# Loads of q, k and v issued by GpSimd and cast by the transfer, in an attention and feed-forward kernel

## The chip, the cores and the metric

The kernel runs on one core of one Trainium2 chip. The metric is the time of one execution on the device in microseconds (us); less is better. The core has five engines that run their own instruction streams in order and meet at semaphores: PE (matrix products), DVE (vector), ACT (activations), POOL (GpSimd) and SP (sync). DMA engines, shared by all of them, move the data; a transfer is issued by an instruction on one of the engines.

## The reference

Eight batches of eight heads, 576 tokens, 64 elements a head. Attention has a bias from a running sum of `s`, a causal mask, and is followed by a layer norm and a two-layer feed-forward block with a residual.

```python
scores = scale * np.matmul(q, k.transpose(0, 1, 3, 2))
cum = np.cumsum(np.maximum(s, 0.0), axis=-1)
bias = -(cum[:, :, :, None] - cum[:, :, None, :])
scores = np.where(causal, -1000000000.0, scores + np.minimum(bias, 0.0))
attn = softmax(scores)
x = np.matmul(attn, v)                      # (8, 8, 576, 64) -> (8, 576, 512)
xn = (x - mu) / np.sqrt(var + 1e-06) * g_ln
out = x + np.maximum(xn @ w_ch1, 0.0) @ w_ch2
```

Inputs and output are float32; inside, the kernel works in bfloat16 for the products.

## The kernel before

The order of all work is written out by hand; nothing reorders it. The main loop runs over 64 heads, n = 8 * batch + head. In each head it does four things: `pre(n)` issues loads, casts and transposes for heads to come; `scores(b, h)` makes the transposed scores of one head with PE (`sa`, `sb`, `sc`), takes their exponential on ACT into `er`, and has POOL zero what the causal mask hides (`affine_select`, four of 128 x 128 a head, and a smaller one for two heads in `scores_d`); `pv` multiplies the exponentials of the head before with `v` into `pot`; and between these stand units of the feed-forward block of the batch before (`run_units`), 32 `ph` and `py` units a batch. The attention stages thus fill in between the large matrix products, and the two share PE.

A head's scores need q and k with the 64 head elements on the partitions. Four heads make a group, numbered gam (two in a batch); a group's q and k lie in `qT[gam % 2]` and `kT[gam % 2]`. Batches 0 and 1 (`NPE` is 2) are loaded by token blocks, cast into tiles of the pool `pairs` and transposed on PE. Batches 2 to 7, groups 4 to 15, go another way, in three steps for k and three for q:

- `ld_rows(kind, gam, part)` loads token rows of four heads as float32 into a staging tile, from the sync queue. Part 0 holds three tiles of 128 tokens; part 1 one of 128 and one of 64.
- `cast_rows` has POOL cast each tile into one of six row buffers, `rows[turn % 6]` (128 tokens x 4 heads x 128 columns of bfloat16), and copy four bias columns beside the 64 elements (from `cTk` or `cTq`).
- `tr_rows` issues one transposing DMA a row buffer from the sync queue, out of `rows` into `kT` or `qT`.

`v` is loaded from the sync queue into `vtmp` and cast by `cast("v", ...)` into `v_bf[b % 2]`, in five tiles a batch, the last of 64 tokens.

The sync queue also issues the weights' loads in the first heads and the stores of `out`. All loads, transposes and stores of batches 2 to 7 therefore stand in the sync queue in the order in which `pre` writes them, and all casts stand in POOL's queue between the selects of the mask. In the steady part, `pre` spreads the three steps over four heads:

```python
elif n >= 16:
    gam = n // 4 + 1
    if n % 4 == 0:
        tr_rows("k", gam, 0)
        cast_rows("q", gam, 0)
        ld_rows("q", gam, 1)
    elif n % 4 == 1:
        tr_rows("q", gam, 0)
        cast_rows("k", gam, 1)
        ld_rows("k", gam + 1, 0)
```

and so on for the two other heads. The feed-forward weights `w2` are cast by POOL at heads 12 to 14 (`cast_w2`), those of `w1` by DVE.

Of the kernel before, what the change touches and what calls it, by code (L numbers as in the profile page):

```python
# [9 lines left out]
F32 = mybir.dt.float32  # L10
BF16 = mybir.dt.bfloat16
# [4 lines left out]
P = 128  # L16
# [3 lines left out]
def kernel(  # L20
# [11 lines left out]
    nc = tc.nc  # L32
    B, H, S, D = q.shape
# [5 lines left out]
    NF = S // P  # L39
    NT = NF + 1  # L40
    TL = S - NF * P
# [4 lines left out]
    EW = 1664  # L46
    G = 4
    NPE = 2
    PARTS = ((0, 1, 2), (3, 4))
    QT = 6  # L50
    QP = S // QT

    const = ctx.enter_context(tc.tile_pool(name="const", bufs=1))
    stage = ctx.enter_context(tc.tile_pool(name="stage", bufs=2))
    pairs = ctx.enter_context(tc.tile_pool(name="pairs", bufs=3))
    wst = ctx.enter_context(tc.tile_pool(name="wst", bufs=4))
    small = ctx.enter_context(tc.tile_pool(name="small", bufs=4))
    xpool = ctx.enter_context(tc.tile_pool(name="xpool", bufs=3))
# [41 lines left out]

    def load_v(b, t):
        pn = P if t < NF else TL
        tmp = stage.tile([P, H, D], F32, name="vtmp", tag="vtmp", bufs=3)
        nc.sync.dma_start(
            out=tmp[:pn], in_=v[b, :, t * P : t * P + pn, :].rearrange("h s d -> s h d")
        )
        return tmp

    def copy_on(eng, out, in_):
        if eng == "act":  # L110
            nc.scalar.copy(out=out, in_=in_)
        elif eng == "dve":
            nc.vector.tensor_copy(out=out, in_=in_)
        else:
            nc.gpsimd.tensor_copy(out=out, in_=in_)  # L115

    loaded = {}
# [10 lines left out]
    def cast(kind, b, i, eng):  # L128
        if b >= B:
            return  # L130
        tmp = loaded.pop((kind, b, i))
        if kind == "v":
            pn = P if i < NF else TL
            copy_on(eng, v_bf[b % 2][:pn, i, :, 0:D], tmp[:pn])
        else:
            t = pairs.tile([P, QT, 2, D], BF16, name=kind + "p", tag=kind + "p")
            copy_on(
                eng,
                t[0:QP].rearrange("p t h d -> p h t d"),
                tmp[0:QP].rearrange("p h (t d) -> p h t d", d=D),  # L140
            )
            ready[kind, b, i] = t
# [45 lines left out]
    def bias_rows():  # L188
# [7 lines left out]
        for t0, t1, pn in ((0, NF, P), (NF, NT, TL)):  # L196
# [5 lines left out]
                out=cTq[0:pn, t0:t1, :, 3], in0=tr[0:pn, 0, t0:t1, :], scalar1=-1.0  # L202
            )

    def ld_rows(kind, gam, part):
        if gam >= 2 * B:
            return
        src = k if kind == "k" else q
        b, h0 = gam // 2, (gam % 2) * G
        tmp = stage.tile([P, 3, G, D], F32, name=kind + "tmp", tag=kind + "tmp")  # L210
        for u, t in enumerate(PARTS[part]):
            pn = P if t < NF else TL
            nc.sync.dma_start(
                out=tmp[0:pn, u],
                in_=src[b, h0 : h0 + G, t * P : t * P + pn, :].rearrange("h s d -> s h d"),
            )
        loaded[kind, gam, part, "rows"] = tmp

    turn = [0]

    def cast_rows(kind, gam, part):
        if gam >= 2 * B:
            return
        tmp = loaded.pop((kind, gam, part, "rows"))
        got = []
        for u, t in enumerate(PARTS[part]):
            pn = P if t < NF else TL
            r = rows[turn[0] % 6]
            turn[0] += 1
            nc.gpsimd.tensor_copy(out=r[0:pn, :, 0:D], in_=tmp[0:pn, u])  # L230
            nc.gpsimd.tensor_copy(
                out=r[0:pn, :, D:KA],
                in_=(cTk if kind == "k" else cTq)[0:pn, t, gam * G : (gam + 1) * G, :],
            )
            got.append((t, pn, r))
        ready[kind, gam, part, "rows"] = got

    def tr_rows(kind, gam, part):
        if gam >= 2 * B:
            return  # L240
        dst = (kT if kind == "k" else qT)[gam % 2].rearrange("p h s -> p (h s)")
        for t, pn, r in ready.pop((kind, gam, part, "rows")):
            nc.sync.dma_start_transpose(  # L243
                out=dst[:, t * G * P : t * G * P + G * pn].rearrange(
                    "p (h s) -> p h s", h=G
                ),
                in_=r[0:pn].rearrange("p h c -> p (h c)"),
            )
# [293 lines left out]
    for i in range(2):  # L542
# [43 lines left out]
    def pre(n):  # L586
        b, h = n // H, n % H
# [74 lines left out]
            if 3 <= h and b + 1 < B:  # L662
                cast("v", b + 1, h - 3, "pool")

        if n == 10:
            ld_rows("k", 4, 0)
        elif n == 11:
            ld_rows("q", 4, 0)
        elif n == 12:
            cast_rows("k", 4, 0)  # L670
            ld_rows("k", 4, 1)
        elif n == 13:
            tr_rows("k", 4, 0)
            cast_rows("q", 4, 0)
            ld_rows("q", 4, 1)
            ld_rows("k", 5, 0)
        elif n == 14:
            tr_rows("q", 4, 0)
            cast_rows("k", 4, 1)
            ld_rows("q", 5, 0)  # L680
        elif n == 15:
            tr_rows("k", 4, 1)
            cast_rows("q", 4, 1)
            tr_rows("q", 4, 1)
            cast_rows("k", 5, 0)
            ld_rows("k", 5, 1)
        elif n >= 16:
            gam = n // 4 + 1
            if n % 4 == 0:
                tr_rows("k", gam, 0)  # L690
                cast_rows("q", gam, 0)
                ld_rows("q", gam, 1)
            elif n % 4 == 1:
                tr_rows("q", gam, 0)
                cast_rows("k", gam, 1)
                ld_rows("k", gam + 1, 0)
            elif n % 4 == 2:
                tr_rows("k", gam, 1)
                cast_rows("q", gam, 1)
                ld_rows("q", gam + 1, 0)  # L700
            else:
                tr_rows("q", gam, 1)
                cast_rows("k", gam + 1, 0)
                ld_rows("k", gam + 1, 1)

    NU = {10: 4, 11: 4, 12: 4, 13: 4, 14: 3, 15: 3, 16: 3, 17: 3, 18: 4}

# [82 lines left out]
```

## Time and profile before

| | |
|---|---|
| timed runs | 470.35, 472.9 and 474.61 us; median 472.9 |
| profiled execution | 468.62 us, of which the span from the first to the last instruction is 466.9 |
| granted PE clock, mean | 0.893 |
| PE, DVE, ACT, POOL busy | 371.4, 213.3, 175.4, 193.2 us |
| DMA | 61.09 MB in 167,578 packets, 155,624 of them under 512 bytes |

A profile comes from one execution. In its lists of groups, a row has the kernel's line, the engine, the operation, what it writes and reads by the program's names, sizes, the count; then the busy time in us and the mean of one in ns; then the time that the engine was idle just before, and what ended it ("issue" where the profile shows nothing that was waited for). A row of the timeline has its start and its length in us, and in brackets the idle time before it in us and what released it. SPq is the sync engine's queue: the time of an instruction there is the time to issue a transfer, not to carry it out. A window row has the busy time of PE, PE's weight loads, DVE, ACT and POOL with instruction counts, then the granted PE clock, the mean busy share of the 16 DMA engines, and GB/s.

### The profile page before, as it was taken

Reading aid. Unit: us, or ns where it says so; the run is one execution under the profiler, and the core shown is the slowest. Engines: PE = TensorE matmul, PEld = TensorE weight load, DVE = VectorE, ACT = ScalarE, POOL = GpSimd, SP = SyncE. Lnnn points to the kernel's source line nnn. Section 1 sums busy time; section 2 is a strip of 40 time slices with the busy share of each in tenths; the row PEclk is TensorE's granted clock in tenths of the full one; section 3 lists DMA queues with packets and bytes.
Section 4 is the critical chain, followed back from the end, with each engine's and each line's share of the span. In section 5 each row is a group of like instructions: output and inputs, shape, how many; then the busy total and the mean of one; then the engine's idle time right before and its main releaser. Section 6 shows DMA issues by size and latency. Waiting matters only on the chain. (4 is left out here: it accounts for less than half of the span.)

```text
span 466.9 us, 8307 instructions
## 1 busy us (share of the span) xinstructions
PE 371.4 (80%) x2848; PEld 200.3 (43%) x2895; DVE 213.3 (46%) x525; ACT 175.4 (38%) x339; POOL 193.2 (41%) x609
## 2 busy tenths in 40 slices
PE   1486469917979984999299939896699899999995
PEld 0264335504535542555155515453355455444442
DVE  7579777523714640447024712473145526511211
ACT  4252225603337242643255325532272463050320
POOL 3274516835646625554446545543466222000000
PEclk9975559987979995999789977999599999999999
DMA  7885078985877487665866586549765600101102
GB/s 201 216 249 138 13 251 241 217 181 137 191 146 139 97 176 169 115 129 119 189 135 132 117 196 131 117 103 174 162 133 107 137 2 22 69 0 46 46 23 68
DMA packets 167578, 61.09 MB, mean 131 GB/s; under 512 B 155624, under 2 KB 158768, under 8 KB 167536
## 3 DMA queue, kind: packets, MB, share of 16 engines
q1 hardware_dynamic: 167456, 60.51, 57.1%
q8 instruction: 23, 0.38, 0.4%
q14 instruction: 19, 0.16, 0.1%
q10 hardware_dynamic: 80, 0.05, 0.0%
HBM read 36.85 MB, written 9.44 MB: 99 GB/s over the span
## 5 line engine op out<-in xcount | busy, mean ns | idle before, releaser
L485 PE MATMUL py<-w_bf,hT 128*128 128x512 bf16 x554 | 135.6, 382 | 1.5 <-DVE yo L494 0.4
L467 PE MATMUL ph<-xT,w_bf 128*128 128x512 bf16 x488 | 130.3, 403 | 2.1 <-ACT hT L477 0.5
L328 POOL TENSOR_SCALAR_AFFINE_SELECT er<-er 128x128 bf16<-128x128 bf16 x256 | 73.4, 303 | 87.4 <-ACT er L314 86.9
L314 ACT ACTIVATE er<-sa 128x512 bf16<-128x512 f32 x64 | 38.1, 596 | 166.1 <-PE sa L305 107.3
L477 ACT ACTIVATE hT<-ph 128x512 bf16<-128x512 f32 x108 | 64.5, 597 | 91.9 <-PE ph L467 90.8
L467 PEld LDWEIGHTS <-w_bf 128*128 128x128 bf16 x576 | 53.9, 101 | 58.1 <-issue 11.3
L475 DVE TENSOR_SCALAR hT<-ph 128x512 bf16<-128x512 f32 x36 | 24.9, 692 | 113.7 <-PE ph L467 112.2
L305 PEld LDWEIGHTS <-kT 68*128 68x128 bf16 x464 | 35.8, 105 | 95.2 <-issue 38.2
L305 PE MATMUL sa<-qT,kT 68*128 68x512 bf16 x64 | 27.8, 434 | 60.2 <-DMA qT<-rows 47.3
L485 PEld LDWEIGHTS <-hT 128*128 128x128 bf16 x576 | 51.9, 98 | 50.2 <-issue 2.0
L379 PEld LDWEIGHTS <-er 128*128 128x128 bf16 x960 | 42.7, 105 | 17.9 <-issue 5.2
L379 PE MATMUL pot<-v_bf,er 128*128 128x65 bf16 x960 | 45.1, 203 | 3.2 <-POOL v_bf L115 2.5
L230 POOL CAST rows<-qtmp 128x256 bf16<-128x256 f32 (+1 forms) x60 | 24.1, 401 | 46.8 <-issue 25.1
L387 DVE RECIPROCAL rinv<-pot 128x5 f32<-128x5 f32 x64 | 12.4, 193 | 61.2 <-PE pot L379 61.0
L494 DVE TENSOR_TENSOR yo<-py,xb 128x512 f32<-128x512 f32 x32 | 22.0, 689 | 39.5 <-PE py L485 39.3
L314 ACT ACTIVATE er<-sc 128x512 bf16<-128x512 f32 x64 | 38.9, 608 | 0.0
L314 ACT ACTIVATE er<-sb 128x512 bf16<-128x512 f32 x64 | 38.2, 596 | 1.8 <-PE sb L305 0.7
L230 POOL CAST rows<-ktmp 128x256 bf16<-128x256 f32 (+1 forms) x60 | 23.9, 399 | 25.7 <-DMA kT<-rows 17.3
L305 PE MATMUL sb<-qT,kT 68*128 68x384 bf16 (+2 forms) x176 | 28.4, 269 | 2.5 <-DMA qT<-rows 2.3
L305 PE MATMUL sc<-qT,kT 68*128 68x256 bf16 (+1 forms) x224 | 28.5, 249 | 0.0
L389 DVE TENSOR_TENSOR xb<-pot,rinv 128x256 f32<-128x256 f32 x64 | 27.2, 424 | 2.2
L438 DVE TENSOR_SCALAR xn<-xb,mv,rs 128x512 bf16<-128x512 f32 x32 | 20.6, 704 | 9.7 <-POOL rs L425 9.7
(71 smaller groups left out, 289.8 us busy)
## 6 DMA issues: line engine op xcount, KB each, us to landing
vtmp<-in_v_dram SPq DMA_DIRECT2D x32, 256.0 KB
out_dram<-yo SPq DMA_DIRECT2D x32, 256.0 KB
ktmp<-in_k_dram SPq DMA_DIRECT2D x48, 128.0 KB
qtmp<-in_q_dram SPq DMA_DIRECT2D x48, 128.0 KB
w1tmp<-in_moe_w_ch_dram SPq DMA_DIRECT2D x8, 512.0 KB
w2tmp<-in_moe_w_ch_dram SPq DMA_DIRECT2D x8, 512.0 KB
ktmp<-in_k_dram SPq DMA_DIRECT2D x8, 288.0 KB
qtmp<-in_q_dram SPq DMA_DIRECT2D x8, 288.0 KB
```

What stands on the lines that cost most here:

```text
L230: nc.gpsimd.tensor_copy(out=r[0:pn, :, 0:D], in_=tmp[0:pn, u])
L305: nc.tensor.matmul(dst[:, a0 - q0 : a1 - q0], lhsT=k_cols(b, h, kb), rhs=cols, start=True, stop=True,)
L314: nc.scalar.activation(out=e[:, u, o : o + 512], in_=a, func=ACT.Exp, scale=scale)
L328: nc.gpsimd.affine_select(out=e[:, u, o : o + P], in_=e[:, u, o : o + P], compare_op=ALU.is_ge, fill=0.0, base=0, pattern=[[1, P]], channe ...
L379: nc.tensor.matmul(pot[:, t, :], lhsT=e[:, u, o : o + P], rhs=vv[:, kb, h, :], start=(kb == 0), stop=(kb == last),)
L389: nc.vector.tensor_tensor(out=xb[b][:, :, hs], in0=pot[:, 0:NF, 0:D], in1=rinv[:, 0:NF].unsqueeze(2).to_broadcast([P, NF, D]), op=ALU.mult,)
L438: nc.vector.tensor_scalar(out=xn, in0=x, scalar1=mv[:, t, 0:1], scalar2=rs[:, t : t + 1], op0=ALU.subtract, op1=ALU.mult,)
L467: nc.tensor.matmul(ph, lhsT=w1_bf[:, kd, fb * P : (fb + 1) * P], rhs=xT[:, kd, :], start=(kd == 0), stop=(kd == KD - 1),)
L475: nc.vector.tensor_scalar_max(out=hT[:, fb, :], in0=ph, scalar1=0.0)
L477: nc.scalar.activation(out=hT[:, fb, :], in_=ph, func=ACT.Relu)
L485: nc.tensor.matmul(py[0], lhsT=hT[:, fb, t * P : (t + 1) * P], rhs=w2_bf[:, fb, :], start=(fb == 0), stop=(fb == FB - 1),)
L494: nc.vector.tensor_add(out=yo, in0=py[0], in1=x)
```

## The change

For batches 2 to 7 the loads of q, k and v are issued by GpSimd, with a float32 source and a bfloat16 destination, so that the transfer itself converts. The destination is the row buffer, or `v_bf`. Staging tiles and POOL's casts of these batches fall away; the bias columns are still copied by POOL, right behind each load. There are nine row buffers instead of six, `pairs` has two buffers instead of three, and a group's steps stand in other heads: k part 0 is loaded six heads before the group's first head, q part 0 five, both parts 1 four heads before; the transposes follow two heads after each load. Before, q part 1 was transposed one head before the group, now two.

```diff
+    NR = 9
-    pairs = ctx.enter_context(tc.tile_pool(name="pairs", bufs=3))
+    pairs = ctx.enter_context(tc.tile_pool(name="pairs", bufs=2))
-    rows = [const.tile([P, G, P], BF16, name=f"rows{i}") for i in range(6)]
+    rows = [const.tile([P, G, P], BF16, name=f"rows{i}") for i in range(NR)]
...
     def load_v(b, t):
         pn = P if t < NF else TL
+        if b >= NPE:
+            nc.gpsimd.dma_start(
+                out=v_bf[b % 2][:pn, t, :, 0:D],
+                in_=v[b, :, t * P : t * P + pn, :].rearrange("h s d -> s h d"),
+            )
+            return None
...
         tmp = loaded.pop((kind, b, i))
+        if tmp is None:
+            return
...
     def ld_rows(kind, gam, part):
-        tmp = stage.tile([P, 3, G, D], F32, name=kind + "tmp", tag=kind + "tmp")
-        for u, t in enumerate(PARTS[part]):
+        got = []
+        for t in PARTS[part]:
             pn = P if t < NF else TL
-            nc.sync.dma_start(
-                out=tmp[0:pn, u],
+            r = rows[turn[0] % NR]
+            turn[0] += 1
+            nc.gpsimd.dma_start(
+                out=r[0:pn, :, 0:D],
                 in_=src[b, h0 : h0 + G, t * P : t * P + pn, :].rearrange("h s d -> s h d"),
             )
-    def cast_rows(kind, gam, part):
-            nc.gpsimd.tensor_copy(out=r[0:pn, :, 0:D], in_=tmp[0:pn, u])
             nc.gpsimd.tensor_copy(
                 out=r[0:pn, :, D:KA],
                 in_=(cTk if kind == "k" else cTq)[0:pn, t, gam * G : (gam + 1) * G, :],
             )
...
+        for gam in range(2 * NPE, 2 * B):
+            m = n - 4 * gam
+            if m == -6:
+                ld_rows("k", gam, 0)
+            elif m == -5:
+                ld_rows("q", gam, 0)
+            elif m == -4:
                 tr_rows("k", gam, 0)
+                ld_rows("k", gam, 1)
                 ld_rows("q", gam, 1)
+            elif m == -3:
                 tr_rows("q", gam, 0)
+            elif m == -2:
                 tr_rows("k", gam, 1)
                 tr_rows("q", gam, 1)
```

The lines of the changed kernel are other ones: the row load is at L226, the bias copy at L230, the transpose at L242, the select at L327, the `v` load at L105.

POOL at head 27 (batch 3, head 3), before: the cast of a `v` tile, three casts of k rows with their bias copies, and the four selects of the head.

```order
L115 CAST v_bf_103<-vtmp 128x8x64
L230 CAST rows_109<-ktmp 128x4x64
L231 COPY rows_109<-cTk 128x4x4
L230 CAST rows_110<-ktmp 128x4x64
L231 COPY rows_110<-cTk 128x4x4
L230 CAST rows_111<-ktmp 128x4x64
L231 COPY rows_111<-cTk 128x4x4
L328 AFFINE_SELECT er<-er 128x128 x4
```

POOL at the same head after the change (here `rows_109` to `rows_117` are the nine buffers):

```order
L105 DMA v_bf_103<-in_v_dram 128x8x64
L226 DMA rows_109<-in_q_dram 128x4x64
L230 COPY rows_109<-cTq 128x4x4
L226 DMA rows_110<-in_q_dram 128x4x64
L230 COPY rows_110<-cTq 128x4x4
L226 DMA rows_111<-in_q_dram 128x4x64
L230 COPY rows_111<-cTq 128x4x4
L327 AFFINE_SELECT er<-er 128x128 x4
```

Each cast has become the issue of a transfer, at the same place ahead of the selects. At head 28, after the change, POOL issues one `v` load and four row loads:

```order
L105 DMA v_bf_103<-in_v_dram 128x8x64
L226 DMA rows_112<-in_k_dram 128x4x64
L230 COPY rows_112<-cTk 128x4x4
L226 DMA rows_113<-in_k_dram 64x4x64
L230 COPY rows_113<-cTk 64x4x4
L226 DMA rows_114<-in_q_dram 128x4x64
L230 COPY rows_114<-cTq 128x4x4
L226 DMA rows_115<-in_q_dram 64x4x64
L230 COPY rows_115<-cTq 64x4x4
L327 AFFINE_SELECT er<-er 128x128 x4
L351 AFFINE_SELECT er<-er 64x2x64
```

Both parts 1 of a group stand in one head. `rows_115` is the buffer that held the same group's first k tile; its transpose stands in the sync queue at this head.

The sync queue at heads 32 and 33, before: stores, transposes and loads stand between each other.

```order
L507 DMA out_dram<-yo 128x512
L243 DMA_TRANSPOSE kT_107<-rows_113 128x4x128
L243 DMA_TRANSPOSE kT_107<-rows_114 128x4x128
L243 DMA_TRANSPOSE kT_107<-rows_109 128x4x128
L213 DMA qtmp<-in_q_dram 128x4x64
L213 DMA qtmp<-in_q_dram 64x4x64
L507 DMA out_dram<-yo 128x512
L104 DMA vtmp<-in_v_dram 128x8x64
L243 DMA_TRANSPOSE qT_105<-rows_110 128x4x128
L243 DMA_TRANSPOSE qT_105<-rows_111 128x4x128
L243 DMA_TRANSPOSE qT_105<-rows_112 128x4x128
```

After the change, at the same heads:

```order
L506 DMA out_dram<-yo 128x512
L242 DMA_TRANSPOSE kT_107<-rows_116 128x4x128
L242 DMA_TRANSPOSE kT_107<-rows_117 128x4x128
L242 DMA_TRANSPOSE kT_107<-rows_109 128x4x128
L506 DMA out_dram<-yo 128x512
L242 DMA_TRANSPOSE qT_105<-rows_110 128x4x128
L242 DMA_TRANSPOSE qT_105<-rows_111 128x4x128
L242 DMA_TRANSPOSE qT_105<-rows_112 128x4x128
```

The loads have left the queue; stores and transposes keep their order.

More of the change, by code (lines that the diff above doesn't have):

```diff
@@ L203, in bias_rows @@
             )
+    turn = [0]
     def ld_rows(kind, gam, part):
@@ L209, in ld_rows @@
         b, h0 = gam // 2, (gam % 2) * G
-        tmp = stage.tile([P, 3, G, D], F32, name=kind + "tmp", tag=kind + "tmp")
-        for u, t in enumerate(PARTS[part]):
+        got = []
+        for t in PARTS[part]:
             pn = P if t < NF else TL
-            nc.sync.dma_start(
-                out=tmp[0:pn, u],
+            r = rows[turn[0] % NR]
+            turn[0] += 1
+            nc.gpsimd.dma_start(
+                out=r[0:pn, :, 0:D],
                 in_=src[b, h0 : h0 + G, t * P : t * P + pn, :].rearrange("h s d -> s h d"),
             )
-        loaded[kind, gam, part, "rows"] = tmp
-    turn = [0]
-    def cast_rows(kind, gam, part):
[L222 to L230, printed above, removed]
             nc.gpsimd.tensor_copy(
@@ L663, in pre @@
                 cast("v", b + 1, h - 3, "pool")
[L665 to L689, printed above, removed]
+        for gam in range(2 * NPE, 2 * B):
[5 more added lines that the diff above has]
+            elif m == -4:
                 tr_rows("k", gam, 0)
-                cast_rows("q", gam, 0)
+                ld_rows("k", gam, 1)
                 ld_rows("q", gam, 1)
-            elif n % 4 == 1:
+            elif m == -3:
                 tr_rows("q", gam, 0)
-                cast_rows("k", gam, 1)
-                ld_rows("k", gam + 1, 0)
-            elif n % 4 == 2:
+            elif m == -2:
                 tr_rows("k", gam, 1)
-                cast_rows("q", gam, 1)
-                ld_rows("q", gam + 1, 0)
-            else:
                 tr_rows("q", gam, 1)
-                cast_rows("k", gam + 1, 0)
-                ld_rows("k", gam + 1, 1)
     NU = {10: 4, 11: 4, 12: 4, 13: 4, 14: 3, 15: 3, 16: 3, 17: 3, 18: 4}
```

## The prediction

> **What bounds the kernel now.** I read the page's first part, then the waits of the tensor engine, of GpSimd (POOL) and of the sync queue (SPq), then one stall in the timeline. The page first.
>
> ```profile
> PE 371.4 (80%) x2848; PEld 200.3 (43%) x2895; DVE 213.3 (46%) x525; ACT 175.4 (38%) x339; POOL 193.2 (41%) x609
> ```
>
> No engine is full over the span. PE, at 80%, is nearest, so the question is what its idle fifth waits for. The waits answer that (engine and line, what was waited for, us in total, times, longest).
>
> ```profile
> PE sa L305 <- DMA qT<-rows: 47.3, 8, 10.2
> POOL rows L230 <- issue: 28.9, 8, 5.6
> POOL rows L230 <- DMA qT<-rows: 20.2, 11, 5.7
> POOL rows L230 <- DMA kT<-rows: 17.3, 8, 3.8
> SPq L243 <- POOL er L328: 34.5, 32, 1.8
> SPq L243 <- POOL rows L231: 30.8, 27, 2.3
> ```
>
> Eight times the first score matmul of a group (`sa`) waits for the transposing DMA that writes `qT`: 47.3 us, the largest wait of PE. The rest shows why that DMA is late: POOL's casts into the six row buffers wait for transposes to read those buffers out, and the sync queue's transposes wait for POOL. Each in-order queue holds up the other. The timeline of one stall, at head 36:
>
> ```profile
> 217.51 0.39 POOL L230 CAST rows<-qtmp 64x256 bf16<-64x256 f32 x1 [4.67 <-issue]
> 221.75 2.82 SPq L243 DMA_TRANSPOSE kT<-rows  x2
> 225.65 0.40 POOL L230 CAST rows<-ktmp 128x256 bf16<-128x256 f32 x1 [2.57 <-DMA kT<-rows]
> 227.42 2.70 SPq L243 DMA_TRANSPOSE qT<-rows  x2
> 231.41 0.58 PE L305 MATMUL sa<-qT,kT 68*128 68x512 bf16 x1 [8.61 <-DMA qT<-rows]
> 232.66 1.90 PE L467 MATMUL ph<-xT,w_bf 128*128 128x512 bf16 x4
> 238.84 0.38 PE L305 MATMUL sa<-qT,kT 68*128 68x512 bf16 x1
> 239.50 1.89 PE L467 MATMUL ph<-xT,w_bf 128*128 128x512 bf16 x8
> 241.17 0.54 POOL L328 TENSOR_SCALAR_AFFINE_SELECT er<-er 128x128 bf16<-128x128 bf16 x2 [0.20 <-ACT er L314]
> 243.41 0.38 PE L305 MATMUL sa<-qT,kT 68*128 68x512 bf16 x1
> 245.86 0.62 PE L379 MATMUL pot<-v_bf,er 128*128 128x65 bf16 x15
> ...
> 267.69 0.38 PE L305 MATMUL sa<-qT,kT 68*128 68x512 bf16 x1
> ...
> 279.46 0.59 PE L305 MATMUL sa<-qT,kT 68*128 68x512 bf16 x1 [7.04 <-DMA qT<-rows]
> ```
>
> Three numbers come from it. From 238.84 (head 37) to 267.69 (head 43) are six heads without a stall, 28.85 us, 4.81 each; eight would take 38.5 us. From stall to stall, 231.41 to 279.46, a batch of eight heads takes 48.05. The difference is more than the 7 to 9 us of waiting, because after a stall PE runs slowly for a while: four `ph` matmuls in 1.90 us at 232.66, eight in 1.89 at 239.50. The head after the stall takes 7.43 us where the next takes 4.57, 2.86 more.
>
> **What the change removes.** POOL loses its casts of rows and of `v` (batches 2 to 7). SPq loses those loads, and with them its waits for staging buffers; transposes and stores stay. Nine row buffers instead of six, and loads two heads ahead of their transposes, take the mutual hold-up apart. A row load now waits for a transpose issued one or two heads earlier, with one exception. The 64-partition `q` load of the third step reuses the buffer whose transpose is issued in the same head. That transpose waits for PE to finish the scores of the head before, then takes about 1.4 us on the queue (2.82 for two) and 1.3 to land (230.12 to 231.41). POOL gets there after its four selects, three loads and three copies, later than that, so this wait costs nothing at the price below. What else could be late at a group's first scores is ten transposes at about 1.35, 13.5 us, in the 19.2 us of four heads: they fit, if rows arrive.
>
> **What it adds: POOL writes the transfers itself.** POOL's rows now:
>
> ```profile
> L328 POOL TENSOR_SCALAR_AFFINE_SELECT er<-er 128x128 bf16<-128x128 bf16 x256 | 73.4, 303 | 87.4 <-ACT er L314 86.9
> L230 POOL CAST rows<-qtmp 128x256 bf16<-128x256 f32 (+1 forms) x60 | 24.1, 401 | 46.8 <-issue 25.1 <-DMA qT<-rows 20.2 <-POOL rows L231 1.5
> L230 POOL CAST rows<-ktmp 128x256 bf16<-128x256 f32 (+1 forms) x60 | 23.9, 399 | 25.7 <-DMA kT<-rows 17.3 <-issue 3.8 <-DMA ktmp<-in_k_dram 3.5
> L115 POOL CAST v_bf<-vtmp 128x512 bf16<-128x512 f32 (+1 forms) x36 | 21.9, 612 | 6.4 <-DMA vtmp<-in_v_dram 6.4
> L231 POOL COPY rows<-cTk 128x16 bf16<-128x16 bf16 (+1 forms) x60 | 13.8, 230 | 0.0
> L231 POOL COPY rows<-cTq 128x16 bf16<-128x16 bf16 (+1 forms) x60 | 11.5, 192 | 0.0
> L352 POOL TENSOR_SCALAR_AFFINE_SELECT er<-er 64x128 bf16<-64x128 bf16 x32 | 9.3, 292 | 5.8 <-ACT er L349 5.8
> L425 POOL TENSOR_TENSOR rs<-rs,mhalf 128x4 f32<-128x4 f32 (+1 forms) x8 | 8.7, 1089 | 25.7 <-DVE rs L424 23.0 <-DMA kT<-rows 2.6
> ```
>
> Per batch POOL keeps 73.4/8 = 9.2 of selects, 9.3/8 = 1.2 of small ones, 8.7/8 = 1.1 of powers and (13.8 + 11.5)/6 = 4.2 of bias copies: 15.7 us. It loses 48.0/6 = 8.0 of row casts and about 5 x 0.61 = 3.0 of `v` casts. It gains 25 transfers: 16 row loads of 128 partitions (512 runs of 256 bytes), 4 of 64, 4 `v` loads of 1,024 runs and one of 512.
>
> What such a transfer costs POOL no row shows, so I bound it. The cheap end is what the sync queue takes to issue the same transfer:
>
> ```profile
> 242.39 1.67 SPq L213 DMA_DIRECT2D ktmp<-in_k_dram  x3
> 226.89 0.43 SPq L104 DMA_DIRECT2D vtmp<-in_v_dram  x1
> ```
>
> That is 0.56 for a row load, 0.43 for `v`. For the dear end I let POOL step through every run at its own pace. A cast of 256 elements takes 401 ns and a copy of 16 about 211, so 0.79 ns an element; four elements a run (two addresses and two lengths, my assumption) give 512 x 4 x 0.79 ns + 0.21 = 1.83 us for a row load, 1.02 for one of 64 partitions, 3.45 and 1.83 for `v`. The nearest row is not evident, so I take the geometric middle: 1.01, 0.76, 1.22 and 0.89. The batch adds 16 x 1.01 + 4 x 0.76 + 4 x 1.22 + 0.89 = 25.0 us, and POOL needs **40.7 us a batch**, against the 38.5 that PE needs. The ends are 13.4 (POOL 29) and 49.0 (POOL 65).
>
> The Trainium skill, page "DMA: Bandwidth & Descriptors", section "Specifications", gives about 1 us to the first byte where GpSimd issues and about 0.6 where sync does. Adding that 0.4 to the sync queue's rows would make the 25 transfers 23.4 us, POOL 39.1 and the median about 426, an estimate; no run here shows it.
>
> Behind a POOL transfer stand the selects of the next head, and PE's `pot` waits for those. The cover: head 37's selects end at 241.71 and its `pot` starts at 245.86, 4.15 us later. Heads 2 to 4 of a batch carry a `v` load and three or four row loads each: 6.3, 6.0 and 7.0 us of POOL, 19.4 in the time of three heads, 14.4. POOL falls 5.0 late, 0.85 more than the cover. I take the batch at 40.7 + 0.85, **41.5 us**.
>
> The first stall, at head 16, is another place:
>
> ```profile
> 105.56 0.59 PE L305 MATMUL sa<-qT,kT 68*128 68x512 bf16 x1 [10.22 <-DMA qT<-rows]
> 85.51 3.98 POOL L172 CAST w_bf<-w2tmp 128x1024 bf16<-128x1024 f32 x4
> ```
>
> It costs 10.2 and a slow head, about 13.1. At head 14 POOL will have the four `w2` casts (3.98), three `v` loads (3.7), three row loads with copies (3.7) and its selects (1.4), 12.7 us in a head of about 4; head 15 adds 1.5. Less the cover, PE loses about 6.3. The gain here is 6.8.
>
> **The sum.** Five batches (heads 20 to 60) save 5 x (48.05 - 41.5) = 32.8, the first stall 6.8: 39.6 us. The profiled execution took 468.62 us (466.9 of span); the result is 429.0. That execution lies 4.3 under the median of the timed runs, 472.9, so I predict **433 us** for a median. The extra memsets of three buffers (0.3 each) and the two-deep `pairs` pool fall where POOL waits for ACT (86.9 us in the L328 row); uncovered they cost 1 us.
>
> **The rivals.**
>
> POOL's transfers are cheap (below 0.85 us a row load). Then PE sets the pace and all 47.3 us go, with about 15 of the slow heads (two thirds of eight times 2.86, since short waits cost less): 406, **410** as a median. For it speaks that the sync queue issues the same in 0.56. Chance 0.14.
>
> POOL becomes the bound, and the kernel is slower. The place is POOL's queue in batches 1 to 6, the price what writing 512 or 1,024 runs takes. It breaks even where the 25 transfers take 48.05 - 0.85 - 15.7 = 31.5 us, that is 1.26 times my price, 1.27 us a row load; above that every batch loses. At the dear end 5 x (65 + 0.85 - 48.05) = 89 us are lost and nothing is won at head 16: **about 560**; halfway from the break-even, about 515. For it speaks that rows are short, and so many for each transfer; against it only that POOL has 59% of the span free. Chance 0.25.
>
> The DMA engines become the bound, because a converting packet takes longer.
>
> ```profile
> q1 hardware_dynamic: 167456, 60.51, 57.1%
> 231.00:276.00 45.00, 40.53 (x330) 22.02 (x336) 19.13 (x53) 20.39 (x40) 23.77 (x80) 0.92 0.67 141
> ```
>
> The last row's 0.67 is the DMA share: 32.2 us of a 48.05 us batch. A packet takes 0.571 x 466.9 x 16 / 167456 = 25.5 ns on the mean. Converted per batch: 9,216 row and 4,608 `v` packets. If these took twice as long, 22 us more over 16 engines, a batch would need 54 us: **about 503**. It binds from 1.4 times on and loses from 1.7. Against it: they write half the bytes. Chance 0.10.
>
> POOL is held up by the vector engine. The vector rows that read SBUF with one source:
>
> ```profile
> L438 DVE TENSOR_SCALAR xn<-xb,mv,rs 128x512 bf16<-128x512 f32 x32 | 20.6, 704 | 9.7 <-POOL rs L425 9.7
> L475 DVE TENSOR_SCALAR hT<-ph 128x512 bf16<-128x512 f32 x36 | 24.9, 692 | 113.7 <-PE ph L467 112.2
> ```
>
> If each `xn` shut POOL out while it runs, a batch would gain 20.6/8 = 2.6 us: 44.1, and **446** in all. But `xn`, from SBUF, takes 704 ns where `hT`, from PSUM, takes 692: it runs no faster from there. Chance 0.04. The rule behind it is in the Trainium skill, page "SBUF — State Buffer", section "SBUF: two separate sides": a vector operation in a two-port mode keeps GpSimd from writing its descriptors, so that a transfer issued there seems blocked. By that rule the change is a risk here only if `xn` is in such a mode, and the two durations speak against it.
>
> Last, gain and cost cancel near the break-even price: no change, **473**, chance 0.07.
>
> **How the numbers follow.** Forecast (415 to 455) 0.40, cheap POOL 0.14, vector hold-up 0.04: faster 0.58. Cancelled: 0.07. POOL bound 0.25 and DMA bound 0.10: slower 0.35. A change of 1% either way is about what a measurement of this kernel can tell from none. The range runs from 409, the floor of the cheap case, to 515, the middle of the bound case; left out is the dear half of POOL's price, some 0.15, and a little below. Faster cases alone run from 409 to 455.
>
> **What would show it.** Right: the 47.3 us wait of `sa` falls under 10; POOL's transfers show 0.8 to 1.2 us for 512 runs; POOL is over 85% busy between heads 20 and 60 with its idle before L327 nearly gone; `pot` has a short new wait for the selects. The cheap rival shows POOL still idle for ACT, and heads of 4.6 to 5.1 us throughout. The bound case shows `pot` waiting for selects in nearly every head and sync's transposes waiting for row loads. The DMA case shows row loads landing late after POOL has long issued them. I am wrong first of all if the price of a POOL transfer lies outside 0.85 to 1.25 us.

## The result, and the profile after

The changed kernel takes 442.94 us (median of three, 441.30 to 445.39) against 472.9: the ratio is 0.938, its 95% interval 0.928 to 0.948. The forecast was 433, with a range of 409 to 515. The ratios here leave out the slower executions that a chip shows now and then, so they can differ by half a per cent from the quotient of two medians. The profiled execution took 441.30 us, 439.2 of span, at a mean granted clock of 0.975.

The first part of its page, and the two large rows of the list of DMA queues (packets, MB, share of 16 engines):

```profile
PE 367.5 (84%) x2848; PEld 199.3 (45%) x2895; DVE 215.0 (49%) x525; ACT 174.7 (40%) x339; POOL 244.1 (56%) x612
...
q0 software_dynamic: 85344, 10.63, 45.7%
q1 hardware_dynamic: 82112, 39.27, 39.4%
```

PE is nearer to full and POOL's time has grown by 51 us, but neither sets the pace alone. The waits (total, times, longest) tell what is left:

```profile
PE pot L378 <- POOL er L327: 7.2, 4, 4.1
PE sa L304 <- DMA qT<-rows: 6.9, 4, 3.0
PE sb L304 <- DMA qT<-rows: 6.1, 6, 2.3
POOL rows L226 <- DMA kT<-rows: 27.5, 8, 5.5
POOL rows L226 <- DMA qT<-rows: 17.2, 4, 5.1
SPq L506 <- DVE yo L493: 71.7, 11, 17.3
SPq L506 <- DVE rinv L386: 48.3, 7, 19.7
```

The 47.3 us of `sa` have become 6.9. POOL's row loads wait 44.7 us for transposes, where its casts waited 37.5 before (20.2 and 17.3). The last two rows are stores of `out`, which sit in the sync queue until the vector engine has their tile `yo` (the second row names another instruction of that engine). Before the change the same two waits were 66.4 us, not 120.0:

```profile
SPq L507 <- DVE rinv L387: 35.9, 7, 20.4
SPq L507 <- DVE yo L494: 30.5, 7, 17.3
```

POOL's groups of rows give the price of a transfer (busy, mean ns, idle before):

```profile
L327 POOL TENSOR_SCALAR_AFFINE_SELECT er<-er 128x128 bf16<-128x128 bf16 x256 | 73.7, 309 | 60.2 <-ACT er L313 59.6
L226 POOL DMA_DIRECT2D rows<-in_q_dram x60 | 43.4, 723 | 28.4 <-DMA kT<-rows 27.5
L226 POOL DMA_DIRECT2D rows<-in_k_dram x60 | 44.0, 733 | 17.5 <-DMA qT<-rows 17.2
L105 POOL DMA_DIRECT2D v_bf<-in_v_dram x30 | 26.0, 866 | 0.0
```

A row load takes 0.73 us of POOL on the mean, a `v` load 0.87; these means include the smaller loads of 64 partitions, and a row load of 128 takes 0.74 to 0.76. The rows of the windows from the first scores of head 20 to those of head 60, before and then after, give the five batches of the sum (start and end, length, then busy PE, PEld, DVE, ACT, POOL, the clock, the DMA share, GB/s):

```profile
131.97:373.03 241.06, 203.37 (x1659) 110.22 (x1689) 99.72 (x275) 101.77 (x200) 119.52 (x400) 0.90 0.67 139
```

```profile
126.07:345.52 219.45, 197.67 (x1660) 108.10 (x1688) 101.16 (x275) 101.70 (x201) 155.43 (x395) 0.97 1.08 115
```

A batch went from 48.21 to 43.89 us: 21.6 us of the gain. 5.9 more come before head 20 (it starts at 126.07 instead of 131.97), 0.2 after head 60. That is all of the 27.7 between the two spans (466.9 and 439.2). Here is the loop that keeps a batch at 43.9, in the timeline from head 31 to 36:

```profile
180.29 2.51 SPq L242 DMA_TRANSPOSE qT<-rows  x2
...
185.46 0.39 PE L304 MATMUL sc<-qT,kT 68*128 68x256 bf16 x4
...
189.79 0.69 DVE L493 TENSOR_TENSOR yo<-py,xb 128x512 f32<-128x512 f32 x1 [0.77 <-PE py L484]
...
190.51 0.34 SPq L506 DMA_DIRECT2D out_dram<-yo  x1
191.01 4.55 SPq L242 DMA_TRANSPOSE kT<-rows  x3
...
194.62 0.62 POOL L226 DMA_DIRECT2D rows<-in_q_dram  x1 [3.94 <-DMA kT<-rows]
...
196.64 1.20 POOL L424 TENSOR_TENSOR rs<-rs,mhalf 128x5 f32<-128x5 f32 x1
...
197.88 2.46 DVE L437 TENSOR_SCALAR xn<-xb,mv,rs 128x512 bf16<-128x512 f32 x4 [1.92 <-POOL rs L424]
...
200.82 0.69 DVE L493 TENSOR_TENSOR yo<-py,xb 128x512 f32<-128x512 f32 x1
...
201.54 0.34 SPq L506 DMA_DIRECT2D out_dram<-yo  x1
...
202.00 3.98 SPq L242 DMA_TRANSPOSE qT<-rows  x3
...
206.99 0.74 POOL L226 DMA_DIRECT2D rows<-in_k_dram  x1 [3.83 <-DMA qT<-rows]
```

A store waits for `yo`; the three transposes behind it start when it is gone, at 191.01, although PE had finished with the old `kT` (the scores of head 31, the `sc` row) at 185.85 and the queue had issued nothing since 182.80. The rows were hardly what was late: POOL had issued their loads by 181.16, and such a load lands 3.7 us after its issue in the median. Then POOL's 64-token row load waits 3.94 us for the first of them; behind that load stand the selects and the power `rs`, for which the vector engine waits; its next `yo`, and with it the next store, comes late, and so do the next transposes. At 214.22 `sa` of head 36 still waits 2.96 us for `qT`.

### The profile page after: what moved, and what is told of

The parts are those of the page before. It is cut to its first block, busy times and chain, and to the rows that moved or that the text cites. A ratio compares the mean times of both kernels' runs of the same rounds, so it can differ in the third digit from the quotient of the medians.

```text
span 439.2 us, 8212 instructions
## 1 busy us (share of the span) xinstructions
PE 367.5 (84%) x2848; PEld 199.3 (45%) x2895; DVE 215.0 (49%) x525; ACT 174.7 (40%) x339; POOL 244.1 (56%) x612
## 3 DMA queue, kind: packets, MB, share of 16 engines
q0 software_dynamic: 85344, 10.63, 45.7%
## 4 chain that ended last, share of the span: by engine, by line
PE 48%; DMA 15%; POOL 14%; DVE 12%; issue 7%; ACT 1%; SPq 1%; POOLq 0%; ACTq 0%
PE ph L466 23%; PE py L484 15%; DMA qT<-rows 10%; POOL er L327 5%; PE pot L378 4%; DMA kT<-rows 4%; POOL rows L226 3%; POOL v_bf L105 3%; PE sb L304 2%; PE sc L304 2%; DVE qT L120 2%; PE sa L304 2%; DVE kT L120 2%; DVE xn L437 1%; DMA w2tmp<-in_moe_w_ch_dram 1%
## 5 line engine op out<-in xcount | busy, mean ns | idle before, releaser
L466 PE MATMUL ph<-xT,w_bf 128*128 128x512 bf16 x488 | 126.5, 394 | 2.1 <-issue 0.4
L327 POOL TENSOR_SCALAR_AFFINE_SELECT er<-er 128x128 bf16<-128x128 bf16 x256 | 73.7, 309 | 60.2 <-ACT er L313 59.6
L313 ACT ACTIVATE er<-sa 128x512 bf16<-128x512 f32 x64 | 38.1, 595 | 138.7 <-PE sa L304 108.8
L466 PEld LDWEIGHTS <-w_bf 128*128 128x128 bf16 x576 | 53.0, 100 | 56.8 <-issue 9.0
L226 POOL DMA_DIRECT2D rows<-in_q_dram x60 | 43.4, 723 | 28.4 <-DMA kT<-rows 27.5
L378 PE MATMUL pot<-v_bf,er 128*128 128x65 bf16 x960 | 47.1, 203 | 8.4 <-POOL er L327 7.2
L226 POOL DMA_DIRECT2D rows<-in_k_dram x60 | 44.0, 733 | 17.5 <-DMA qT<-rows 17.2
L313 ACT ACTIVATE er<-sb 128x512 bf16<-128x512 f32 x64 | 38.1, 595 | 4.8 <-PE sb L304 4.8
L304 PE MATMUL sb<-qT,kT 68*128 68x384 bf16 (+2 forms) x176 | 27.5, 262 | 6.1 <-DMA qT<-rows 6.1
L453 PE MATMUL trx<-ident,xn 128*128 128x128 bf16 x144 | 14.7, 229 | 20.2 <-DVE xn L437 9.5
L304 PE MATMUL sc<-qT,kT 68*128 68x256 bf16 (+1 forms) x224 | 27.7, 243 | 0.0
```

The source lines that it names most:

```text
L226: nc.gpsimd.dma_start(out=r[0:pn, :, 0:D], in_=src[b, h0 : h0 + G, t * P : t * P + pn, :].rearrange("h s d -> s h d"),)
L304: nc.tensor.matmul(dst[:, a0 - q0 : a1 - q0], lhsT=k_cols(b, h, kb), rhs=cols, start=True, stop=True,)
L313: nc.scalar.activation(out=e[:, u, o : o + 512], in_=a, func=ACT.Exp, scale=scale)
L327: nc.gpsimd.affine_select(out=e[:, u, o : o + P], in_=e[:, u, o : o + P], compare_op=ALU.is_ge, fill=0.0, base=0, pattern=[[1, P]], channe ...
L378: nc.tensor.matmul(pot[:, t, :], lhsT=e[:, u, o : o + P], rhs=vv[:, kb, h, :], start=(kb == 0), stop=(kb == last),)
L466: nc.tensor.matmul(ph, lhsT=w1_bf[:, kd, fb * P : (fb + 1) * P], rhs=xT[:, kd, :], start=(kd == 0), stop=(kd == KD - 1),)
```

## The experiments

Each run is timed against the kernel before on the same chip (medians 470.4, 471.78 and 470.89 in the three groups); "a batch" is a fifth of the time from the first scores of head 20 to those of head 60. The groups ran on different chips, and these medians differ by 1.4 us; a difference between runs of two groups is no surer than that.

### Which wait is left

**One load later.** The third step's q loads move behind the transposes of q part 0, one head later, so that no load reuses a buffer transposed in its own head.

```diff
                 ld_rows("k", gam, 1)
-                ld_rows("q", gam, 1)
             elif m == -3:
                 tr_rows("q", gam, 0)
+                ld_rows("q", gam, 1)
```

> The changed kernel, but q part 1 of each group is loaded three heads before the group instead of four, so that POOL no longer waits in the same head for the transpose of the group's first k tile. Theory A (what is left of the stalls begins with that wait: POOL stands 3.7 us, the power for the layer norm, the selects and the next loads stand behind it): the waits of POOL's row loads for transposes fall from 44.7 us to under 15, the batch from 44 us to 39.5 to 41, the median from 443 to 422 to 430. Theory B (the DMA engines are full, since a converting packet takes 38 ns, and transposes land late for that): no change, 440 to 446. Theory C (stores ahead of transposes in the sync queue): little, 436 to 443.

Measured: 433.69 us (431.53 to 437.31), ratio 0.921 (0.915 to 0.928), outside the ranges of all three cases.

```profile
POOL rows L226 <- DMA qT<-rows: 9.4, 4, 3.5
POOL rows L226 <- DMA kT<-rows: 2.3, 1, 2.3
PE sa L304 <- DMA qT<-rows: 11.1, 5, 3.3
```

POOL's 44.7 us of waits fall to 11.7, but the profiled batch stays at 43.8 (43.9 without the edit). What that execution gains (437.31 against 441.30; it was the slowest of four) lies ahead of head 20, which starts at 121.17 instead of 126.07, and `sa` waits for `qT` longer than before the edit. Taking the load out of the loop does not make the transposes early.

**Ten row buffers** do the same by size, at the price of one staging tile of `v`.

```diff
-    NR = 9
+    NR = 10
-        tmp = stage.tile([P, H, D], F32, name="vtmp", tag="vtmp", bufs=3)
+        tmp = stage.tile([P, H, D], F32, name="vtmp", tag="vtmp", bufs=2)
```

> The changed kernel with ten row buffers instead of nine (room taken from the staging of v in the first two batches, two buffers instead of three): each load reuses the buffer that held the same tile of the group before, whose transpose was issued two heads ago. Nothing else moves. Theory A: as in the run with the later q load, the waits for transposes under 15 us, 422 to 430. Theory B: 440 to 446. If the smaller staging of v costs something it shows before head 16.

Measured: 431.49 us (428.44 to 433.90), ratio 0.916 (0.909 to 0.923), just above theory A's range; a batch 42.1. POOL's waits shrink to 7.3, `sa` still waits 9.6 us for `qT`, so again the transposes themselves are late. The lost staging tile costs 15.0 us of POOL's casts of `v` in the first batches, so the size of this gain is not clear.

**Stores later.** Every store of `out` is collected and issued behind the transposes of the next head.

```diff
+    stores = []
+    def flush():
+        while stores:
+            o, y = stores.pop(0)
+            nc.sync.dma_start(out=o, in_=y)
...
-                nc.sync.dma_start(out=out[b, t * P : (t + 1) * P, :], in_=yo)
+                stores.append((out[b, t * P : (t + 1) * P, :], yo))
...
         pre(n)
+        flush()
```

> The changed kernel, but each store of out is put into the sync queue behind the next head's transposes instead of ahead of them. Theory C (sync stands at a store that waits for the vector engine while transposes behind it are ready): the wait of sa for qT disappears, 425 to 432. Theory A: POOL's wait for the k transpose stays, because that transpose waits for PE's scores all the same; a gain of 0 to 8 us, 435 to 443. Theory B: 440 to 446.

Measured: **411.49 us** (410.96 to 412.21), ratio 0.874 (0.869 to 0.878): theory C's mechanism, but 13.5 us under its range. No score matmul waits for `qT<-rows` any more. The waits that are left, and the window from head 20 to head 60:

```profile
POOL rows L226 <- DMA kT<-rows: 9.2, 5, 5.3
SPq L508 <- DVE yo L493: 32.4, 9, 17.3
```

```profile
126.32:316.21 189.89, 188.13 (x1660) 105.40 (x1688) 97.84 (x275) 99.70 (x200) 155.07 (x395) 1.00 1.34 134
```

This row and that of the changed kernel are the pair to read. POOL is busy 155.07 us here and 155.43 there: the same work. PE is busy 99% of the time, at full clock, where it was 90% at 0.97. A batch takes 37.98 instead of 43.89: the order of the stores costs 29.6 us in five batches. 20.0 of them are idle time of PE (21.78 against 1.76 us), the other 9.5 the same matmuls taking longer.

**Stores later in the kernel before.** The same edit, without the change.

```diff
-                nc.sync.dma_start(out=out[b, t * P : (t + 1) * P, :], in_=yo)
+                stores.append((out[b, t * P : (t + 1) * P, :], yo))
...
         pre(n)
+        flush()
```

> The kernel before (loads on the sync queue, casts on POOL, six row buffers), with each store of out put behind the next head's transposes in the sync queue. Theory C2 (the store that stands ahead of the transposes is what stalled the kernel before as well; taking loads off the sync queue matters little): 415 to 435. Theory D (before, the mutual hold-up of POOL's casts and sync's transposes over six buffers is a stall of its own, as the prediction has it): 455 to 472.

Measured: 452.84 us (451.05 to 454.25), ratio 0.964 (0.955 to 0.973), between the two ranges and 2 us under theory D's. `sa` still waits for `qT`, 30.5 us in 8 times, and POOL's casts wait for transposes:

```profile
PE sa L305 <- DMA qT<-rows: 30.5, 8, 10.0
POOL rows L230 <- DMA kT<-rows: 24.3, 15, 5.5
POOL rows L230 <- DMA qT<-rows: 21.1, 15, 3.0
```

So the order of the stores is worth 19 us without the change and about 30 with it (441.30 and 410.96 us in the profiled executions). Without the change, the mutual hold-up of casts and transposes that the prediction describes is still there.

### Which part of the change does it

**Nine buffers and the new heads alone.** Loads stay on the sync queue and POOL's casts stay; only the buffers and the steps' heads are those of the change.

```diff
             if m == -6:
                 ld_rows("k", gam, 0)
             elif m == -5:
+                cast_rows("k", gam, 0)
                 ld_rows("q", gam, 0)
...
-            nc.gpsimd.dma_start(
-                out=r[0:pn, :, 0:D],
+            nc.sync.dma_start(
+                out=tmp[0:pn, u],
```

> The nine buffers and the earlier heads of the changed kernel, but with the loads on the sync queue into float32 staging and POOL's casts as before; v as before. If the gain is one of timing and buffers alone: 435 to 450. If it comes from taking loads off the sync queue and casts off POOL: no gain, 460 to 480, with sync's transposes still waiting for POOL and for staging.

Measured: 465.31 us (463.84 to 466.64), ratio 0.987 (0.981 to 0.993), in the range of the second case; a batch 48.6. What POOL waits for has only changed its name:

```profile
POOL rows L233 <- DMA ktmp<-in_k_dram: 77.9, 25, 10.5
POOL rows L233 <- issue: 45.6, 7, 8.9
PE pot L382 <- POOL er L331: 20.3, 13, 3.0
```

With room in the row buffers the casts wait for their loads, which stand in the sync queue behind transposes and stores; PE waits for the selects behind the casts.

**The same with stores later** (the edit shown above).

```diff
         pre(n)
+        flush()
```

> The earlier heads and nine buffers of the changed kernel, loads on the sync queue, casts on POOL, v as before, and the stores behind the next head's transposes. If stores and timing are all that counts: 410 to 420, as with GpSimd's loads. If POOL's casts, which wait in POOL's queue for loads to land, and loads in the sync queue cost PE time of their own: 440 to 465.

Measured: 456.44 us (454.01 to 458.88), ratio 0.972 (0.962 to 0.983), in the range of the second case. POOL's wait for `ktmp` is still 73.2 us in 23 times. Neither buffers nor stores nor both give what the change gives, as long as the loads stand in that queue in this order. Whether another order of the sync queue would do as well was not tried.

**GpSimd issues, POOL casts.** From there one word is changed: the row loads are issued by GpSimd, still as float32 into the staging tiles. `v` stays on the sync queue.

```diff
-            nc.sync.dma_start(
+            nc.gpsimd.dma_start(
                 out=tmp[0:pn, u],
```

> Stores behind the next head's transposes; row loads are issued by GpSimd, but as float32 into the staging tiles, and POOL casts them; v as before the change, from the sync queue. Compared with the run that has the same steps with row loads on the sync queue (456.4) and the one whose row loads convert (415.4). My theory, that the loads gain by leaving the sync queue, where they stand behind transposes: POOL's waits for ktmp fall from 73 to under 20 us and the time to 415 to 430, as 8 us of casts a batch still fit under 38. Rival, that it is the conversion, which spares the staging buffers and the wait for landing: 445 to 460, POOL waits for ktmp of 50 us or more. Packets of the row loads: 18 to 20 ns median if converting is what made them 32, and about 30 if it is GpSimd's queue.

Measured: 438.99 us (437.26 to 443.62), ratio 0.933 (0.927 to 0.939), between the two ranges.

```profile
POOL rows L233 <- DMA ktmp<-in_k_dram: 4.3, 8, 0.8
POOL rows L233 <- DMA qtmp<-in_q_dram: 10.5, 14, 1.3
PE pot L382 <- POOL er L331: 11.0, 10, 2.3
```

The theory's wait is right (73.2 falls to 4.3, 14.8 with `qtmp`), but its time is not: with casts and issues both on POOL, `pot` waits 11.0 us for the selects. Leaving the sync queue is worth 17.5 us here (456.44 to 438.99, on two chips).

The Trainium skill, page "DMA: Bandwidth & Descriptors", section "Issuing engines are not separate DMA queues", says that issuing from another engine saves only the issuing time, which is usually small. Here the one word took 17.5 us, and what fell with it is POOL's wait for loads that stood behind transposes and stores.

The question of the packets stays open: the float32 loads went out as 4,096-byte packets, 3,456 of them, which are not the 256-byte packets that I wanted to compare. The one word thus changed the packets too, but it did not spare the DMA engines anything: the sync queue's packets took 58.6% of 452.9 us before it and 47.7% of 435.5 after, 57.7 us less of each engine, and GpSimd's took 13.8% of 435.5, 60.1 us. Whether single loads also land sooner in this form was not separated from the queue.

**Only q and k converted, `v` as before, stores later.**

```diff
-        if b >= NPE:
-            nc.gpsimd.dma_start(
-                out=v_bf[b % 2][:pn, t, :, 0:D],
...
-            return None
```

> The changed kernel with the stores later, but v loaded from the sync queue into staging and cast by POOL as before; only q and k rows are loaded and cast by GpSimd's transfers. If v's part of the change matters (five loads a batch in the sync queue ahead of transposes, waiting for staging, and casts on POOL that wait for them): 416 to 430. If only the rows matter: 409 to 414.

Measured: 415.44 us (414.45 to 417.29), ratio 0.884 (0.875 to 0.893), just under the range for `v`; a batch 38.3. Conversion in the row loads, which spares POOL their casts and the staging tiles, is the step from 439.0 to 415.4. That of `v` is worth some 4 us (415.4 against 411.5, on two chips), little of it in the steady batches (38.3 against 38.0).

### What POOL's price decides

The rival in which POOL sets the pace asks for dearer transfers. I made them dearer with more copies of the same bias columns behind each row load, stores later, so that no other wait is in the way. First six copies instead of one.

```diff
+            for _ in range(6):
                 nc.gpsimd.tensor_copy(
                     out=r[0:pn, :, D:KA],
```

> The kernel with the stores later, but POOL makes each bias copy six times (the same bytes), to make a row load dearer for POOL: five more copies of about 0.17 us for each of 20 row loads, 17 us a batch. POOL is busy 29.6 us of a batch of 38.1 with single copies. If POOL's work sets the pace once it exceeds PE's, as the rival of the prediction has it: batches of about 46.6 us and 450 to 465. If POOL's selects have cover enough, or the copies overlap: 411 to 425.

Measured: 559.56 us (558.67 to 561.16), ratio 1.192 (1.182 to 1.202): missed by 95 us. The price was mis-sized. A row load with one copy takes POOL 0.89 us from load to load, with six 2.54:

```profile
230.65 0.76 POOL L226 DMA_DIRECT2D rows<-in_k_dram  x1
231.40 0.21 POOL L230 COPY rows<-cTk 128x16 bf16<-128x16 bf16 x1
231.54 0.74 POOL L226 DMA_DIRECT2D rows<-in_k_dram  x1
```

```profile
262.35 0.76 POOL L226 DMA_DIRECT2D rows<-in_k_dram  x1
263.10 1.50 POOL L231 COPY rows<-cTk 128x16 bf16<-128x16 bf16 x6
264.89 0.74 POOL L226 DMA_DIRECT2D rows<-in_k_dram  x1 [0.29 <-issue]
```

Here a single copy delays the next load by 0.13 us in all, as that load starts before the copy has ended; of six, the further ones follow one another, and the next load starts 0.29 us behind the last. Then two copies, and four.

```diff
+            for _ in range(2):   # four in the other run
                 nc.gpsimd.tensor_copy(
                     out=r[0:pn, :, D:KA],
```

> Stores behind the next head's transposes, and each bias copy on POOL made twice. One more copy cost about 0.32 us in the run with six, so 20 of them add 6.4 us a batch. POOL is busy 29.8 us of a 38 us batch with the stores later. My theory, that PE sets the pace as long as POOL needs less than PE's 38.1: 411 to 418 us, batches 38 to 39. Rival, that POOL's price shows in the time as soon as it grows, because the selects come later: 6.4 x 6 = 38 more, about 450.

> The same with each bias copy made four times: 60 more copies a batch, about 19 us. My theory: POOL's 29.8 + 19 = 49 us pass PE's 38.1, and POOL sets the pace with its waits on top: batches 49 to 53 us, 470 to 495 us in all, about where the kernel before stands, so that a price of about 1 us more a transfer is the break-even. Rival, that the pace changes only where waits of POOL for transposes are added: below 440.

Measured: two copies 443.41 us (442.36 to 443.92), ratio 0.941 (0.938 to 0.943); four copies 501.89 us (500.48 to 502.05), ratio 1.065 (1.062 to 1.068). Both lie above my numbers, the first near the rival's 450. The timeline of the run with two copies says why:

```profile
251.41 0.76 POOL L226 DMA_DIRECT2D rows<-in_k_dram  x1
252.16 0.47 POOL L231 COPY rows<-cTk 128x16 bf16<-128x16 bf16 x2
252.93 0.74 POOL L226 DMA_DIRECT2D rows<-in_k_dram  x1 [0.30 <-issue]
```

The second copy costs 0.63 us a load (1.52 from load to load), not the 0.32 that I had divided out of six. With the prices as the timelines show them (for four copies, loads at 287.67 and 289.70), taking the 155.07/5 = 31.0 us that POOL is busy in a batch with one copy, and 20 loads:

| copies | load to load, us | POOL needs a batch, us | measured batch, us |
|---|---|---|---|
| 1 | 0.89 | 31.0 | 37.98 |
| 2 | 1.52 | 31.0 + 20 x 0.63 = 43.6 | 43.06 |
| 4 | 2.03 | 31.0 + 20 x 1.14 = 53.8 | 53.45 |
| 6 | 2.54 | 31.0 + 20 x 1.65 = 64.0 | 63.73 |

The batch is the larger of PE's 38.0 and what POOL needs, within 0.6 us. The prices were read after the results, so this is an account and not a forecast. My theory holds with its price corrected. By the rival's reading, that POOL's price shows as soon as it grows, two copies would have made the batch 38.0 + 12.6 = 50.6 us, and it took 43.06. By the same sum the first 0.35 us a load (7 us over 20 loads) are free; no run lies in that stretch. By a straight line between two and four copies, the time of the kernel before, 470.9, is reached at 0.87 us more a load.

### The two orders together

Stores later, and the q loads one head later.

```diff
                 ld_rows("k", gam, 1)
-                ld_rows("q", gam, 1)
             elif m == -3:
                 tr_rows("q", gam, 0)
+                ld_rows("q", gam, 1)
...
         pre(n)
+        flush()
```

> The changed kernel with two moves together: each store of out stands behind the next head's transposes, and q part 1 is loaded one head later. My theory: with the stores behind, PE is 99% busy in the steady batches (38.1 us each), so moving q part 1 can win only at the start, where POOL waited 5.3 us for a kT transpose at head 12; expected 405 to 411 us, steady batches unchanged at 38. Rival, that POOL's waits for transposes still cost PE in the steady batches: under 403. If the later load is too late for its transpose: above 416, with sa waiting for qT again.

Measured: **407.37 us** (407.05 to 407.85), ratio 0.865 (0.863 to 0.867), as my theory had it. A batch takes 38.1, as without the later load; the 4 us come from before head 20 (122.47 instead of 126.32), where POOL's wait for `kT` at head 12 fell from 5.33 us to 1.94. It is the fastest kernel of this study.

## Why the prediction was right or wrong

**Right: the large wait, and what took its place.** `sa`'s 47.3 us are 6.9, under the 10 forecast. The gain ahead of head 20 was put at 6.8 and is 5.9. The wait that should replace the stall at head 16 is there: PE loses 4.08 us to POOL's selects (6.3 forecast; its terms as written give 6.1). But head 16 itself starts only 1.26 us earlier (104.30 against 105.56), and 4.6 us come between heads 16 and 20, so the size is met partly by luck.

```profile
101.56 1.25 PE L378 MATMUL pot<-v_bf,er 128*128 128x65 bf16 x15 [4.08 <-POOL er L327]
```

**Mis-sized: POOL's price.** The geometric middle gave 25.0 us a batch for 25 transfers. Measured are (43.4 + 44.0 + 26.0)/6 = 18.9; a row load of 128 partitions costs 0.74 to 0.76 and not 1.01, a `v` load 0.90 in the median and not 1.22. For a row load the nearest row was the cheap end, the sync queue's 0.56. POOL is busy 31.1 us a batch (155.43/5), not 40.7, so it isn't the bound, and "over 85% busy with its idle before L327 nearly gone" is wrong too: 71%, and 60.2 us over the whole span (87.4 before). The estimate that the prediction works out from the Trainium skill, page "DMA: Bandwidth & Descriptors", section "Specifications", 23.4 us, is also above the measured 18.9; the page's figure is for the first byte and not for what an issue takes of POOL.

**Failed: "so this wait costs nothing at the price below", and "they fit, if rows arrive".** I compared POOL's arrival with PE's finished scores, one transpose and its landing. I left out what stands ahead of that transpose in the sync queue: a store of `out`, which waits for `yo`, although the rows of that queue were before me. At head 32 it holds the transposes from 185.85 to 191.01. POOL does wait there, 44.7 us in all, and since the power and the selects stand behind that load, the wait feeds the next store. The same store is missing from the count of ten transposes, 13.5 us in 19.2, and this is the omission that cost the time: with the load one head later POOL's wait is nearly gone, but the batch is as long (43.8) and the transposes are still late; with the stores behind the transposes the batch is 38.0. The order of the stores is thus shown to be the cause, and the load that I had judged is one link of its loop.

**The sum.** Five batches at 41.5 were to take 207.5 us and took 219.45: 12.0 of the 12.3 us between 429.0 and 441.3. The two errors pull against each other. With POOL's true price PE alone would bound the batch at 38.0 (3.5 better than 41.5); the store order adds 5.9. That the time came out within 3% of the forecast is luck: one term was too dear and another was missing.

**The rivals.** Cheap POOL had the right condition (below 0.85 us) and nearly its time, 410, but only after an edit that it didn't name: 411.5 with stores later. POOL as the bound is real as a mechanism (the table above) and its dear end, about 560 at 65 us of POOL a batch, was met by six copies, which need 64.0; the kernel lies on the cheap side, with 7 us a batch to spare once the stores are moved. The DMA rival was to bind from 1.4 times 25.5 ns a packet. From the page the converting queue takes 0.457 x 439.2 x 16 / 85344 = 37.6 ns, 1.5 times that. Yet it binds nothing: with stores later PE is 99% busy beside it. The vector rival is not the price of a transfer: the `v` load at 197.81, with `xn` beside it from 197.88, takes 0.94 us where the median of all is 0.90 and the longest 0.945. But POOL's selects do feel something there (last section).

## What to carry to other kernels

Before you cost a wait at nothing, write down everything ahead of the releasing instruction in its in-order queue, and what that waits for: here a store stood ahead of the transposes and cost 29.6 us in five batches, where the change brought 21.6. In a queue that issues both stores and what the next stage needs, put the stores behind. An engine with spare time can take on issues until its need for a batch reaches that of the bound (38 us here), and by the four runs of the table every microsecond beyond counts in full.

## What the runs showed of the hardware

- What an issue from GpSimd costs POOL grows much less than the number of runs: 0.62 us for 256 runs of 256 bytes, 0.74 to 0.76 for 512, 0.90 in the median for `v` loads, most of which have 1,024.
- Four selects beside `xn` take POOL 1.66 us, four a few us earlier or later 1.01 and 1.04 (a window row: start and end, length, POOL's busy time in selects, clock, DMA share, GB/s). The prediction took 704 against 692 ns as a sign that `xn` holds up nothing; that was no test of it. What slows the selects was not tested.

```profile
198.78:200.44 1.66, 1.66 (x4) 1.00 0.81 52
207.87:208.91 1.04, 1.03 (x4) 1.00 1.31 164
195.37:196.38 1.01, 1.01 (x4) 1.00 0.85 141
```

- The DMA share of the profile is not a limit at 1: it is 1.34 with stores later, with PE 99% busy. So the times of packets overlap on an engine, and 37.6 ns a packet need not be 37.6 ns taken from the others.
- GpSimd's float32 row loads went out in 4,096-byte packets and took 13.8% of the 16 engines' span of 435.5 us, 60.1 us of each; the converting row loads, half the bytes in 57,216 packets, took 31.0% of 415.6, 128.8 us (the runs with float32 rows and with only q and k converted; `v` on the sync queue in both). How much of this is conversion and how much the smaller packets was not separated.

```profile
q0 software_dynamic: 5376, 14.16, 13.8%
q0 software_dynamic: 57216, 7.09, 31.0%
```
